# Another order of blocks, slots and banks at the two ends of a weighted expert stage

## Chip, cores, metric

One Trainium2 chip, one of its cores. The metric is the device time of one launch in microseconds (us). All arithmetic is float32.

## What is computed

An attention block gives `x` (4352 rows, 128 columns); then a layer of eight experts is applied to it, each weighted by a Sinkhorn-normalised routing matrix `P`:

```
logits = x @ w_gate;  P = exp(logits - max);  8 rounds of row and column normalisation
for e in range(E):                      # E = 8, F = 1024
    h = np.maximum(x @ w1[e], 0.0)
    ye = h @ w2[e]
    out += P[:, e:e + 1] * ye
```

The change touches only the experts, and of them only the later part, which works on inputs already multiplied by `P`.

## The kernel before

The kernel runs three stages: attention; a first expert stage under which the routing is computed (lines 772, 774, 787, 836 of the profile); and, from about 188 us on, the function `weighted()`, which the change edits.

**Groups, items, halves.** `wgroups` cuts the rows into seven groups of `2n` rows: n is 320, 480, 480, 352, 320, 224, 224. Groups 5 and 6 are the same rows; group 5 has six experts, group 6 (`LAST`, in `whole`) has the seventh alone. An item is one group with one expert, 40 in all; each is worked in two halves `s` (t counts the halves: item 0 is t = 0 and 1, group 5 is t = 66 to 77, group 6 is t = 78 and 79).

**First layer, `firsts(t)`.** `product(...)` (line 1158) issues four 64x64 matmuls, one for each quadrant of TensorE. Item 0 uses plain 2x2 blocks: four blocks of `h`, two products each, and a relu on ScalarE (line 1171) behind each block. All later items use seven products (a fast 2x2 scheme): three are copied out by ScalarE (lines 1241, 1246, 1250), three blocks are made by VectorE with an add and relu in one instruction that reads PSUM and a copy (line 1174: h0, then h2, then h3), the fourth, h1, by a ScalarE relu. Products alternate between two PSUM tiles, `pair0` and `pair1`; a product that begins a tile anew waits until its last reader is done.

**Sums of h.** For the second layer's fast scheme VectorE makes four sums, in this order: `ts0 = h3 - h0` (line 1216), `ts1 = h3 - h1` (1219), `ts2 = h1 - ts0` (1220), `ts3 = h2 - ts2` (1221). In item 0 all four stand behind the last block.

**Second layer, `seconds(t)`.** `into(...)` (line 1304) accumulates seven pairs of matmuls, four at a time, in seven slots. `tiles(rho, m, r)` is the part of row half `rho` for PSUM bank `m`: m = 0 reads h0 and h2, m = 1 reads h1 and ts0, m = 2 reads ts1 and ts2, m = 3 reads ts3. The two row halves walk the banks in different orders, so that they never stand in one bank in one slot:

```
order = ((0, 0, 2, 2, 1, 1, 3), (1, 1, 3, 0, 0, 2, 2))
```

So ts1, ts2 and ts3 are all read in slot 2 by one row half or the other.

**How the two are woven.** TensorE's order is written out: one product of `firsts(t)`, one slot of `seconds(t - 1)`, and so on; slot 0 of half t - 1 stands behind product 1 of half t, and slot 6 behind product 0 of half t + 1. VectorE, ScalarE and GpSimd each run their instructions in the order in which the program emits them; loads and stores are issued by SyncE in order.

**Small helpers around the change.** `turn` (line 1354) copies one column of a bank on ScalarE, and so makes ScalarE wait for TensorE. `aside` runs GpSimd's work for the coming items (lines 1071, 1079, 985 and others) and takes up to two pieces of work from the list `leisure`; `spare` lets VectorE take a piece in the gaps behind ts0 and behind ts3. `leisure` holds the sums that finish the previous group (`finish_seven`: eleven additions on line 1445, and two transposes with their stores, lines 1473 and 738). `ended(g, m)` copies a finished bank into `z` (line 1376); `swap_half` sends halves of `z` to the other partitions by DMA (line 1390), `begin_next_to_last` adds the near half of `z` into the result with three VectorE instructions (line 1403), `finish_next_to_last` adds the far half on GpSimd (line 1412) and once on VectorE (line 1413). Group 6 then ends the kernel: its last matmuls (line 1316), the additions on lines 1483 and 1489, transposes on 1498.

Of the kernel before, what the change touches and what calls it, by code (L numbers as in the profile page):

```python
# [14 lines left out]
Alu = mybir.AluOpType  # L15
# [37 lines left out]
def kernel(  # L53
# [12 lines left out]
    nc = tc.nc  # L66
# [14 lines left out]
    H2 = DM // 2  # L81
# [1029 lines left out]
    def weighted():  # L1111
# [14 lines left out]
        for t in range(len(todo)):  # L1126
            if t:
                a0, a1, a2, a3, a4, a5, a6 = turns[-1]
                f0, f1, f2 = unused
                now = [f0, f2, a0, a1, f1, a4, a3] if t == 1 else [f0, f1, f2, a0, a1, a4, a3]  # L1130
                unused = [a2, a5, a6]
            else:
                now, unused = unused[:7], unused[7:]
            turns.append(now)
# [7 lines left out]
        def firsts(t):  # L1142

            i, s = todo[t]
            g, e = witems[i]
            n = wgroups[g][1]
            a, c = pairs[::-1] if t % 2 and i else pairs
            w1, xf = forms[i][0], sources[i]
            h, ts = rooms(t)
            pa, pc = a[:, :, 0:n], c[:, :, 0:n]  # L1150
            p1, p5, u2 = (copies[:, m, 0:2 * n] for m in range(3))

            def product(out, form, x, start, stop):
                for r in range(2):
                    rows = slice(H2 * r, H2 * (r + 1))
                    for col in range(2):
                        o = P * s + H2 * col
                        nc.tensor.matmul(out[H2 * col:H2 * (col + 1), r], w1[rows, PLACE[form], o:o + H2], xf[rows, x],  # L1158
                                         start=start, stop=stop, tile_position=(H2 * r, H2 * col), skip_group_check=True)

            coming = next_of(i, 2) if s else None

            def fetch(lo, hi):
                if coming is not None and coming not in fresh:
                    load_first(coming, lo, hi)

            def add(out, x, y):
                nc.vector.tensor_tensor(flat(out, n), x, flat(y, n), op=Alu.add)

            def relu(x, y):  # L1170
                nc.scalar.activation(out=x, in_=y, func=Act.Relu)  # L1171

            def add_relu(out, x, y):
                nc.vector._custom_dve(TENSOR_ADD_SAT, out=flat(out, n), in0=x, in1=flat(y, n), s0=math.inf, s1=0.0)  # L1174

            def leave(engine, anywhere=False):
                if leisure and leisure[0] is None:
                    leisure.pop(0)
                elif leisure and (anywhere or leisure[0][1]):
                    leisure.pop(0)[0](engine)  # L1180
                    return True

            def gate(x, y):
                nc.scalar.copy(x, y)

            def aside(y):
# [12 lines left out]
                if s == 0 and 0 < i in fresh:  # L1199
                    store_first(i)  # L1200
                if g == 0:
                    pass
                elif chores and (s or not leisure):
                    chores.pop(0)[1]()
                else:
                    for _ in range(2 if g + 2 >= LAST else 1):
                        leave(nc.gpsimd)

            def spare(spot):
                if s == 1 and i + 1 < len(witems):  # L1210
                    sum_x(i + 1, 1 + spot)
                if 0 < g < LAST and (s == 0 or g + 1 == LAST and leisure and leisure[0] and not leisure[0][1]):
                    leave(nc.vector, True)

            def first_of_h():
                nc.vector.tensor_tensor(ts[0], h[3], h[0], op=Alu.subtract)  # L1216

            def sums_of_h():
                nc.vector.tensor_tensor(ts[1], h[3], h[1], op=Alu.subtract)  # L1219
                nc.vector.tensor_tensor(ts[2], h[1], ts[0], op=Alu.subtract)  # L1220
                nc.vector.tensor_tensor(ts[3], h[2], ts[2], op=Alu.subtract)  # L1221

            if i == 0:
                for out, (fi, ti), b in ((pa, (0, 1), 0), (pc, (1, 0), 1), (pa, (1, 1), 2), (pc, (0, 0), 3)):
                    for k in range(2):
                        product(out, 2 * k + fi, 2 * k + ti, k == 0, True)
                        yield
                        if k:
                            relu(flat(h[b], n), out)
                        if b == 0 and k:  # L1230
                            aside(h[b][:, 0:1])
                        if b == 3 and k:
                            first_of_h()
# [16 lines left out]
            nc.scalar.copy(flat(u2, n), pa)  # L1250
# [12 lines left out]
            yield  # L1263
            fetch(4, 6)
            add_relu(h[3], pc, p1)
            if g not in whole:
                first_of_h()
            spare(0)
            yield
            product(pa, 3, 7, False, True)  # L1270
            yield
            fetch(6, 7)
            relu(flat(h[1], n), pa)
            if g not in whole:
                sums_of_h()
            spare(1)
            yield

        def seconds(t):
# [20 lines left out]

            def into(rho, m, half, w, x, r):
                rows = slice(H2 * rho, H2 * (rho + 1))
                c = counts[g, m, half] = counts.get((g, m, half), 0) + 1
                nc.tensor.matmul(acc[g][m][H2 * half:H2 * (half + 1), 0:n], w[rows], flat(x, n)[rows, r],  # L1304
                                 start=c == 1, stop=True, tile_position=(H2 * rho, H2 * half),
                                 skip_group_check=True)

# [36 lines left out]
                                               ((form, 1), ts[2]))[2 * m:2 * m + 2]):  # L1344
                    into(rho, m, half, f[0](*f[1:], r), x, r)

            order = ((0, 0, 2, 2, 1, 1, 3), (1, 1, 3, 0, 0, 2, 2))
            for at in range(7):
                for rho in range(2):
                    m = order[rho ^ t % 2][at]  # L1350
                    tiles(rho, m, order[rho ^ t % 2][:at].count(m))
                yield
                for m in {1: (0, 1) if t == 0 else (0,), 3: (2,)}.get(at, ()):
                    nc.scalar.copy(turn, acc[g][m][:, 0:1])  # L1354
                for part_ in {4: (0,), 5: (1,), 6: (2, 3)}.get(at, ()):
                    fetch(part_)
                if last:
                    for m in {4: (0,), 5: (1,), 6: (2, 3)}.get(at, ()):
                        ended(g, m)
                    if at == 5:  # L1360
                        swap_half(g, 0)
                    if at == 5 and g + 1 == LAST:
                        begin_next_to_last(g)
                    if at == 6:
                        swap_half(g, 1)
                        (finish_next_to_last if g + 1 == LAST else finish_seven)(g)
                yield

        ends, swapped, loading = {}, [], [True]

        def ended(g, m):
# [4 lines left out]
            nc.scalar.copy(ends[g][:, m], acc[g][m][:, 0:n])  # L1376

        def swap_half(g, q):

# [286 lines left out]
```

## Time and profile before

| | |
|---|---|
| median of 3 runs | 888.25 us (888.14 to 888.47) |
| profiled execution, its own time | 888.43 us |
| span of the profile | 886.7 us |
| TensorE busy with matmuls | 879.2 us |
| VectorE busy | 721.7 us |
| ScalarE busy | 387.0 us |
| GpSimd busy | 259.8 us |

The span is the time from the first to the last instruction that the profile records; the rest of the execution's time, 1.7 us, lies outside it. In all rows PE is TensorE's matmuls, PEld its weight loads, DVE is VectorE, ACT ScalarE, POOL GpSimd, and SPq the DMA issues of SyncE. A row of a timeline gives the start in the span, the duration, the engine, the line of the kernel, the operation with output and inputs, the shape and the number of merged instructions; in brackets stands how long the engine had been idle before, and what ended that. One fp32 matmul shows as two records, so a product of four matmuls, or a slot, shows as x8.

### The profile page before, as it was taken

How to read it: one execution, taken by the hardware profiler on the slowest of the kernel's cores; microseconds unless marked ns; L12 is line 12 of the kernel's file. 1: busy time of each engine (PE TensorE's matmuls, PEld its weight loads, DVE VectorE, ACT ScalarE, POOL GpSimd, SP SyncE). 2: the span in 40 equal slices, each digit the busy share in tenths (PEclk: the TensorE clock that was granted, in tenths of full speed). 3: DMA queues.
4: the chain of work that ended last, by engine and by line, in shares of the span. 5: the costliest groups of instructions: out<-in, count | busy, mean ns of one | idle time of the engine just before them, and what ended most of it. 6: DMA issues, size and time to landing. Idle time of an engine off the chain costs nothing.

```text
span 886.7 us, 26215 instructions
## 1 busy us (share of the span) xinstructions
PE 879.2 (99%) x10828; PEld 568.1 (64%) x10828; DVE 721.7 (81%) x981; ACT 387.0 (44%) x817; POOL 259.8 (29%) x253
## 2 busy tenths in 40 slices
PE   9999999999999999999999999999999999999998
PEld 6788656855867656666555555555444566667786
DVE  8699689977888877788877778888788888888986
ACT  3455557544444533333343333334344344445443
POOL 3131125353532213222222222221333333311411
PEclk9999999999999999999999999999999999999999
DMA  8889399786666554454435444434755557566671
GB/s 262 266 272 280 78 232 246 123 261 178 197 190 197 175 167 129 136 142 123 127 99 145 137 125 126 122 107 114 191 146 160 148 133 223 147 181 194 199 209 36
DMA packets 120887, 149.08 MB, mean 168 GB/s; under 512 B 52288, under 2 KB 79808, under 8 KB 120384
## 3 DMA queue, kind: packets, MB, share of 16 engines
q1 hardware_dynamic: 112656, 136.92, 54.4%
q0 software_dynamic: 6720, 10.19, 5.8%
q8 instruction: 86, 1.41, 0.7%
q10 hardware_dynamic: 1392, 0.28, 0.2%
q14 instruction: 33, 0.27, 0.1%
HBM read 104.86 MB, written 25.99 MB: 148 GB/s over the span
## 4 chain that ended last, share of the span: by engine, by line
PE 97%; DVE 2%; ACT 0%; issue 0%; POOL 0%; DVEq 0%; ACTq 0%; POOLq 0%
PE s L1304 38%; PE pair L1158 38%; PE a L772 9%; PE s L836 7%; PE a L336 1%; PE a L465 1%; PE a L120 1%; PE a L306 0%; DVE hb L1221 0%; DVE hb L1219 0%; DVE hb L1220 0%; PE s L375 0%; PE a L429 0%; PE s L395 0%; DVE hb L1216 0%; PE s L1316 0%
## 5 line engine op out<-in xcount | busy, mean ns | idle before, releaser
L1158 PE MATMUL pair<-xf,w1x 64*64 64x320 f32 (+3 forms) x4496 | 570.2, 466 | 0.6 <-DVE hb L1174 0.6
L1304 PE MATMUL s<-hb,w 64*64 64x480 f32 (+3 forms) x2544 | 368.2, 466 | 0.1
L1158 PEld LDWEIGHTS pair<-xf,w1x 64*64 64x64 f32 x4496 | 250.3, 133 | 120.2 <-issue 77.5
L1174 DVE CUSTOM_DVE_ANT_0 hb<-pair,copies 128x960 f32<-128x960 f32 (+3 forms) x234 | 214.7, 918 | 101.8 <-PE pair L1158 92.5
L1304 PE MATMUL s<-hb,ws 64*64 64x480 f32 (+3 forms) x1888 | 286.8, 469 | 1.5 <-DVE hb L1221 1.0
L1304 PEld LDWEIGHTS s<-hb,w 64*64 64x64 f32 x2544 | 152.9, 133 | 78.1 <-issue 51.8
L1304 PEld LDWEIGHTS s<-hb,ws 64*64 64x64 f32 x1888 | 115.0, 133 | 61.4 <-issue 37.9
L1071 POOL TENSOR_TENSOR xf<-xT,pb 128x960 f32<-128x960 f32 (+3 forms) x40 | 70.0, 1750 | 245.5 <-ACT turn L1354 186.9
L1079 POOL TENSOR_TENSOR xf<-xf 128x960 f32<-128x960 f32 (+3 forms) x39 | 68.0, 1743 | 229.1 <-ACT turn L1354 168.4
L1171 ACT ACTIVATE hb<-pair 128x640 f32<-128x640 f32 (+3 forms) x86 | 66.4, 772 | 136.7 <-PE pair L1158 136.0
L772 PE MATMUL a<-xT,w 128*64 128x416 f32 (+3 forms) x512 | 122.9, 465 | 0.0
L1354 ACT COPY turn<-s 128x1 f32<-128x1 f32 x157 | 24.5, 156 | 155.0 <-PE s L1304 154.8
L774 ACT ACTIVATE hb<-a 128x416 f32<-128x416 f32 (+3 forms) x128 | 59.5, 468 | 65.8 <-PE a L772 60.6
L1216 DVE TENSOR_TENSOR hb<-hb 128x960 f32<-128x960 f32 (+3 forms) x78 | 75.1, 963 | 12.8 <-ACT hb L1171 4.9
L1221 DVE TENSOR_TENSOR hb<-hb 128x960 f32<-128x960 f32 (+3 forms) x78 | 72.5, 930 | 8.4 <-DVE hb L1220 0.5
L1219 DVE TENSOR_TENSOR hb<-hb 128x960 f32<-128x960 f32 (+3 forms) x78 | 73.2, 938 | 2.8 <-ACT hb L1171 1.3
L1250 ACT COPY copies<-pair 128x960 f32<-128x960 f32 (+3 forms) x78 | 59.8, 767 | 35.5 <-PE pair L1158 35.5
L1246 ACT COPY copies<-pair 128x960 f32<-128x960 f32 (+3 forms) x78 | 60.0, 770 | 33.1 <-PE pair L1158 33.1
L1241 ACT COPY copies<-pair 128x960 f32<-128x960 f32 (+3 forms) x78 | 59.8, 767 | 32.8 <-PE pair L1158 28.9
L1220 DVE TENSOR_TENSOR hb<-hb 128x960 f32<-128x960 f32 (+3 forms) x78 | 71.9, 922 | 0.0
L836 PE MATMUL s<-hb,ws 128*64 128x416 f32 (+3 forms) x224 | 71.6, 474 | 0.0
L787 DVE TENSOR_TENSOR hb<-hb 128x416 f32<-128x416 f32 (+7 forms) x84 | 57.2, 684 | 12.6 <-ACT hb L774 9.7
(203 smaller groups left out, 659.0 us busy)
## 6 DMA issues: line engine op xcount, KB each, us to landing
w1x<-w1x SPq DMA_DIRECT2D x87, 256.0 KB, 3.4
w<-w2x SPq DMA_DIRECT2D x71, 256.0 KB, 3.2
ws<-w2x SPq DMA_DIRECT2D x35, 256.0 KB, 3.3
pb<-pT SPq DMA_DIRECT2D x14, 480.0 KB, 3.8
xf<-xf SPq DMA_DIRECT2D x28, 240.0 KB, 3.3
w1x<-w1x SPq DMA_DIRECT2D x7, 896.0 KB, 5.9
ws<-w2x SPq DMA_DIRECT2D x36, 128.0 KB, 3.4
pb<-pT SPq DMA_DIRECT2D x13, 320.0 KB, 3.7
```

The lines of the kernel that those rows point to most:

```text
L772: nc.tensor.matmul(ph[sl], loaded_w[j][0][:, P * f + H2 * s:P * f + H2 * (s + 1)], xT[:, at + lo:at + hi], start=True, stop=True, tile_pos ...
L836: nc.tensor.matmul(sums[g][i][H2 * s:H2 * (s + 1)], w, x, start=c == 1, stop=c == per, tile_position=(0, H2 * s))
L1071: nc.gpsimd.tensor_tensor(xf[:, 0:2].rearrange("p b n -> p (b n)"), xT[:, lo:lo + 2 * n], weights.pop(i), op=Alu.mult)
L1079: nc.gpsimd.tensor_tensor(xf[:, 4:6], xf[:, 1:4:2], xf[:, 0:2], op=Alu.subtract)
L1158: nc.tensor.matmul(out[H2 * col:H2 * (col + 1), r], w1[rows, PLACE[form], o:o + H2], xf[rows, x], start=start, stop=stop, tile_position=(H ...
L1171: nc.scalar.activation(out=x, in_=y, func=Act.Relu)
L1174: nc.vector._custom_dve(TENSOR_ADD_SAT, out=flat(out, n), in0=x, in1=flat(y, n), s0=math.inf, s1=0.0)
L1216: nc.vector.tensor_tensor(ts[0], h[3], h[0], op=Alu.subtract)
L1219: nc.vector.tensor_tensor(ts[1], h[3], h[1], op=Alu.subtract)
L1220: nc.vector.tensor_tensor(ts[2], h[1], ts[0], op=Alu.subtract)
L1221: nc.vector.tensor_tensor(ts[3], h[2], ts[2], op=Alu.subtract)
L1304: nc.tensor.matmul(acc[g][m][H2 * half:H2 * (half + 1), 0:n], w[rows], flat(x, n)[rows, r], start=c == 1, stop=True, tile_position=(H2 * r ...
```

## The change

Three edits, all in `weighted()`.

1. In item 0 the blocks of `h` come in the order h3, h0, h1, h2 (before: h0, h1, h2, h3), and each sum stands right behind the last block that it needs: ts0 behind h0, ts1 and ts2 behind h1, ts3 behind h2. The buffers of t = 1 are assigned anew to suit.
2. A group with `2n <= 512` that is not in `whole` (only group 5) takes the slots in the plain order 0, 0, 1, 1, 2, 2, 3 in both row halves. Each row half has two banks of its own, in which two of the `m` lie side by side; the two are added when the group ends: `ended` copies one bank of 2n columns on ScalarE and adds the other to it on VectorE (a new instruction on line 1394 of the changed kernel). The `turn` copies are left out in these groups, and the loads of the next weights (`fetch`) come as soon as the plain order is done with the old ones.
3. In group 5 `spare` lets VectorE take only transposes from `leisure`; the additions are left to GpSimd.

```diff
-                now = [f0, f2, a0, a1, f1, a4, a3] if t == 1 else [f0, f1, f2, a0, a1, a4, a3]
+                now = [f1, a4, f0, f2, a0, a1, a3] if t == 1 else [f0, f1, f2, a0, a1, a4, a3]
...
-                if 0 < g < LAST and (s == 0 or g + 1 == LAST and leisure and leisure[0] and not leisure[0][1]):
+                if 0 < g < LAST and (leisure and leisure[0] and not leisure[0][1] if g + 1 == LAST else s == 0):
                     leave(nc.vector, True)
...
-                for out, (fi, ti), b in ((pa, (0, 1), 0), (pc, (1, 0), 1), (pa, (1, 1), 2), (pc, (0, 0), 3)):
+                for out, (fi, ti), b in ((pa, (0, 0), 3), (pc, (0, 1), 0), (pa, (1, 0), 1), (pc, (1, 1), 2)):
...
-                        if b == 0 and k:
-                            aside(h[b][:, 0:1])
-                        if b == 3 and k:
-                            first_of_h()
-                            sums_of_h()
-                            for part_ in (() if s else (1, 2)):
-                                sum_x(1, part_)
+                            if b == 3:
+                                aside(h[b][:, 0:1])
+                            for do in {0: (first_of_h,), 1: (next_of_h,), 2: (last_of_h,)}.get(b, ()):
+                                do()
+                            if b == 2:
+                                for part_ in (() if s else (1, 2)):
+                                    sum_x(1, part_)
...
-                c = counts[g, m, half] = counts.get((g, m, half), 0) + 1
-                nc.tensor.matmul(acc[g][m][H2 * half:H2 * (half + 1), 0:n], w[rows], flat(x, n)[rows, r],
+                bank_ = (2 * rho + m // 2, half) if narrow(g) and g not in whole else (m, half)
+                c = counts[(g, *bank_)] = counts.get((g, *bank_), 0) + 1
+                out_ = acc[g][m][:, 0:n]
+                if narrow(g) and g not in whole:
+                    out_ = acc[g][2 * rho + m // 2][:, n * (m % 2):n * (m % 2 + 1)]
+                nc.tensor.matmul(out_[H2 * half:H2 * (half + 1)], w[rows], flat(x, n)[rows, r],
...
-            order = ((0, 0, 2, 2, 1, 1, 3), (1, 1, 3, 0, 0, 2, 2))
+            order = ((0, 0, 1, 1, 2, 2, 3),) * 2 if narrow(g) else ((0, 0, 2, 2, 1, 1, 3), (1, 1, 3, 0, 0, 2, 2))
+            full = [max(k for line in order for k in range(7) if line[k] == m) for m in range(4)]
...
-                for m in {1: (0, 1) if t == 0 else (0,), 3: (2,)}.get(at, ()):
-                    nc.scalar.copy(turn, acc[g][m][:, 0:1])
-                for part_ in {4: (0,), 5: (1,), 6: (2, 3)}.get(at, ()):
-                    fetch(part_)
+                if not narrow(g):
+                    for m in {1: (0, 1) if t == 0 else (0,), 3: (2,)}.get(at, ()):
+                        nc.scalar.copy(turn, acc[g][m][:, 0:1])
+                for m in range(4):
+                    if full[m] == at:
+                        fetch(m)
+                        if last:
+                            ended(g, m)
                 if last:
-                    for m in {4: (0,), 5: (1,), 6: (2, 3)}.get(at, ()):
-                        ended(g, m)
-                    if at == 5:
-                        swap_half(g, 0)
-                    if at == 5 and g + 1 == LAST:
-                        begin_next_to_last(g)
+                    for q in range(2):
+                        if at == max(full[2 * q:2 * q + 2]):
+                            swap_half(g, q)
+                            if q == 0 and g + 1 == LAST:
+                                begin_next_to_last(g)
...
-            nc.scalar.copy(ends[g][:, m], acc[g][m][:, 0:n])
+            if not narrow(g):
+                nc.scalar.copy(ends[g][:, m], acc[g][m][:, 0:n])
+            elif m % 2:
+                z = ends[g][:, m - 1:m + 1].rearrange("p m n -> p (m n)")
+                nc.scalar.copy(z, acc[g][m // 2][:, 0:2 * n])
+                nc.vector.tensor_tensor(z, acc[g][2 + m // 2][:, 0:2 * n], z, op=Alu.add)
```

More of the change, by code (lines that the diff above doesn't have):

```diff
@@ L1216, in first_of_h, with next_of_h, last_of_h @@
                 nc.vector.tensor_tensor(ts[0], h[3], h[0], op=Alu.subtract)
-            def sums_of_h():
+            def next_of_h():
                 nc.vector.tensor_tensor(ts[1], h[3], h[1], op=Alu.subtract)
                 nc.vector.tensor_tensor(ts[2], h[1], ts[0], op=Alu.subtract)
+            def last_of_h():
                 nc.vector.tensor_tensor(ts[3], h[2], ts[2], op=Alu.subtract)
             if i == 0:
-                for out, (fi, ti), b in ((pa, (0, 1), 0), (pc, (1, 0), 1), (pa, (1, 1), 2), (pc, (0, 0), 3)):
+                for out, (fi, ti), b in ((pa, (0, 0), 3), (pc, (0, 1), 0), (pa, (1, 0), 1), (pc, (1, 1), 2)):
                     for k in range(2):
@@ L1274, in firsts @@
             if g not in whole:
-                sums_of_h()
+                next_of_h()
+                last_of_h()
             spare(1)
@@ L1352, in seconds @@
                 yield
-                for m in {1: (0, 1) if t == 0 else (0,), 3: (2,)}.get(at, ()):
-                    nc.scalar.copy(turn, acc[g][m][:, 0:1])
-                for part_ in {4: (0,), 5: (1,), 6: (2, 3)}.get(at, ()):
-                    fetch(part_)
-                if last:
-                    for m in {4: (0,), 5: (1,), 6: (2, 3)}.get(at, ()):
-                        ended(g, m)
-                    if at == 5:
-                        swap_half(g, 0)
-                    if at == 5 and g + 1 == LAST:
-                        begin_next_to_last(g)
+                if not narrow(g):
[6 more added lines that the diff above has]
+                            ended(g, m)
+                if last:
+                    for q in range(2):
[3 more added lines that the diff above has]
+                                begin_next_to_last(g)
                     if at == 6:
-                        swap_half(g, 1)
                         (finish_next_to_last if g + 1 == LAST else finish_seven)(g)
@@ L1369, in weighted, with narrow @@
         ends, swapped, loading = {}, [], [True]
+        def narrow(g):
+            return 2 * wgroups[g][1] <= 512
         def ended(g, m):
```

## The prediction

> **What bounds the kernel now.** I read the page first: where the time is, and what the chain that ended last is made of.
>
> ```profile
> PE 879.2 (99%) x10828; PEld 568.1 (64%) x10828; DVE 721.7 (81%) x981; ACT 387.0 (44%) x817; POOL 259.8 (29%) x253
> PE 97%; DVE 2%; ACT 0%; issue 0%; POOL 0%; DVEq 0%; ACTq 0%; POOLq 0%
> ```
>
> TensorE sets the end, and the change neither adds nor removes one matmul. All that it can win is the time in which TensorE stands still or half filled. The chain says who causes that: VectorE. So I went to the chain in the stretch of item 0 (start, duration, what).
>
> ```profile
> 193.84 0.84 DVE hb L1216
> 194.70 1.31 DVE hb L1219
> 196.01 1.28 DVE hb L1220
> 197.32 1.24 DVE hb L1221
> 198.60 0.49 PE s L1304 x2
> ...
> 207.32 0.77 PE s L1304 x8
> 208.09 0.54 PE pair L1158 x8
> ...
> 213.47 0.53 PE pair L1158 x7
> ```
>
> From 208.09 to 213.47 ten undisturbed pieces (products and slots in turn) take 5.38 us, 0.538 each. Before that the four sums run one behind the other, and a slot starts only when the last is done, at 198.60 and again at 207.32. Three rows of the timeline more, for the start of item 0 and its relus, and three of GpSimd:
>
> ```profile
> 188.47 5.64 PE L1158 MATMUL pair<-xf,w1x 64*64 64x320 f32 x80
> ...
> 190.92 0.70 ACT L1171 ACTIVATE hb<-pair 128x640 f32<-128x640 f32 x1 [0.32 <-PE pair L1158]
> ...
> 191.97 1.55 POOL L1079 TENSOR_TENSOR xf<-xf 128x640 f32<-128x640 f32 x1 [3.23 <-DMA xf<-xf]
> 192.02 0.70 ACT L1171 ACTIVATE hb<-pair 128x640 f32<-128x640 f32 x1 [0.40 <-PE pair L1158]
> ...
> 193.10 0.70 ACT L1171 ACTIVATE hb<-pair 128x640 f32<-128x640 f32 x1 [0.37 <-PE pair L1158]
> ...
> 194.60 0.73 POOL L985 TENSOR_TENSOR w1x<-w1x 128x256 f32<-128x256 f32 x1 [1.08 <-DMA w1x<-in_moe_w_dram]
> 195.29 1.31 POOL L984 TENSOR_TENSOR w1x<-w1x 128x256 f32<-128x256 f32 x1
> ```
>
> Slot 2 behind the second half of item 0 starts at 207.32. Ahead of it lie, from 188.47, 20 products (8 of t = 0, 8 of t = 1, 4 of t = 2) and 9 slots (7 and 2). That is 29 pieces x 0.538 = 15.60 us, and 18.85 went by: **3.25 us are lost in item 0**.
>
> Group 5 the same way, with the timeline around its first slot, its last halves, and the places where it stumbles:
>
> ```profile
> 807.53 0.56 PE L1304 MATMUL s<-hb,w 64*64 64x224 f32 x8
> ...
> 821.16 0.86 POOL L1445 TENSOR_TENSOR w<-w,z 64x320 f32<-64x320 f32 x1
> ...
> 821.58 0.62 DVE L1174 CUSTOM_DVE_ANT_0 hb<-pair,copies 128x448 f32<-128x448 f32 x1 [0.20 <-PE pair L1158]
> ...
> 822.10 0.87 POOL L1445 TENSOR_TENSOR m<-m,w 64x320 f32<-64x320 f32 x1
> 822.31 1.13 DVE L1216 TENSOR_TENSOR hb<-hb 128x448 f32<-128x448 f32 x1
> ...
> 831.56 1.31 DVE L1445 TENSOR_TENSOR z<-m,f 64x320 f32<-64x320 f32 x1
> 832.91 1.16 DVE L1174 CUSTOM_DVE_ANT_0 hb<-pair,copies 128x448 f32<-128x448 f32 x2
> ...
> 865.18 2.03 DVE L1174 CUSTOM_DVE_ANT_0 hb<-pair,copies 128x448 f32<-128x448 f32 x3 [0.54 <-ACT turn L1354]
> ...
> 866.34 0.56 PE L1304 MATMUL s<-hb,w 64*64 64x224 f32 x8
> ...
> 869.37 0.56 PE L1304 MATMUL s<-hb,w 64*64 64x224 f32 x8
> ...
> 869.96 0.38 DVE L1083 TENSOR_TENSOR xf<-xf 128x224 f32<-128x224 f32 x1
> ...
> 873.93 0.73 PE L1304 MATMUL s<-hb,w 64*64 64x224 f32 x6
> ```
>
> From 866.34 to 869.37 lie eight pieces, 0.379 each. From slot 0 of the group's first half (807.53) to slot 0 of group 6 (873.93) lie 12 halves x 14 = 168 pieces, 63.6 us; 66.4 went by: **2.8 us are lost in group 5**. A half with no piece of `leisure` keeps VectorE from 865.18 to 870.34, 5.16 us, and TensorE's 14 pieces take 5.30. So an odd half leaves VectorE 0.14 us, and any addition of line 1445 makes it late; the worst place is the addition of 1.31 us at 831.56, which holds back the add-relu at 832.91.
>
> **The change part by part.**
>
> *Item 0.* The sums are the same four for each half, in the same order; only their places move. ts0 may start behind h0's relu (190.92 + 0.70 = 191.62), ts1 and ts2 behind h1's (192.72), ts3 behind h2's (193.80). Slot 0 now starts at 193.85 without ts0 late, and slot 2 is due four pieces later, at 196.0; it wants ts1 and ts2, then ts3 at about 196.1. Alone (0.84 each, row of 193.84) the sums would end at 195.2, no wait. But GpSimd works from 191.97 on, and beside it the same sums took 1.24 to 1.31. Taking GpSimd's turns as they come: ts0 to 192.5, ts1 behind line 1079 to 194.7, ts2 behind line 985 to 196.0, ts3 behind line 984 to about 197.1: a wait of 1.0. Bounds: 0 and 1.7 (all four at 1.31 and one more turn). The second half has over two pieces more to spare and should not wait; one relu there waits for slot 4, which has just been reading the buffer, and is early enough. So **-2.25** (-3.25 to -1.55).
>
> *Group 5.* Four additions go from VectorE to GpSimd, which then does eleven of 0.87 in a group of 66 us; its own queue has room. Two transposes stay. The plain order asks for h1 and ts0 in slot 2, ts1 and ts2 in slot 4, ts3 in slot 6: ts3 gets four slots, 3.0 us, more than in slot 2. What stays is one VectorE sum held up for about 0.5 us (1.13 at 822.31 for 0.62) in each half with two additions on GpSimd, of which there are now four, not two; behind an odd half this leaves the next add-relu 0.4 late. The pair that it frees is wanted two pieces and a product later, so I leave 0.3 us of the 2.8. **-2.5** (-2.8 to -1.7). For matmuls that share a bank by columns, and row halves that read the same operand, no row of slots stands here; line 1158 runs both row halves on the same x at the same 0.379, so I take nothing for it. Leaving out `turn`, and earlier weight loads, cost nothing: ScalarE is 44% busy. Stores of group 4 go out later on SyncE's queue, between loads that are two items ahead; without that cover a store would hold the queue for a transpose, half a microsecond.
>
> *Into group 5.* The second row half now starts in bank 2, not bank 1. The rows below show the copies of banks 2 and 3 at 807.37; bank 2 is free near 807.8, and its matmuls are due at 807.72. **+0.15** (0 to 0.4).
>
> *Out of group 5.* Here something new stands in VectorE's queue.
>
> ```profile
> 807.37 0.76 ACT L1376 COPY z<-s 128x320 f32<-128x320 f32 x2
> ...
> 869.62 0.53 ACT L1250 COPY copies<-pair 128x448 f32<-128x448 f32 x1 [0.22 <-PE pair L1158]
> ...
> 870.48 2.06 DVE L1174 CUSTOM_DVE_ANT_0 hb<-pair,copies 128x448 f32<-128x448 f32 x3
> ...
> 871.11 0.36 PE L1304 MATMUL s<-hb,ws 64*64 64x224 f32 x2
> ...
> 872.80 0.56 PE L1158 MATMUL pair<-xf,w1x 64*64 64x224 f32 x8
> ...
> 873.47 3.21 SPq L1390 DMA_DIRECT2D w<-z  x4
> 873.48 1.18 DVE L1403 TENSOR_TENSOR kept<-kept,z 64x224 f32<-64x224 f32 x3 [0.95 <-ACT z L1376]
> ...
> 874.26 0.14 PEld L1304 LDWEIGHTS s<-hb,w 64*64 64x64 f32 x2 [0.18 <-ACT z L1376]
> ...
> 878.60 0.66 POOL L1412 TENSOR_TENSOR m<-m,w 128x224 f32<-128x224 f32 x1
> ...
> 880.04 0.39 DVE L1489 TENSOR_TENSOR kept<-kept,w 128x224 f32<-128x224 f32 x1 [0.23 <-POOL w L1412]
> ...
> 881.11 0.39 DVE L1483 TENSOR_TENSOR kept<-s,kept 128x224 f32<-128x224 f32 x1 [0.38 <-PE s L1316]
> ```
>
> In the plain order the first half of `z` is complete behind slot 3, not slot 5. In the changed program VectorE therefore has, between the add-relus of h2 and h3 of t = 78, the new addition of two banks and the three instructions of line 1403, which used to stand behind h3. Slot 3 ends at 871.47 (last row at 871.11 + 0.36). The copy of 448 columns takes 0.53 (as on line 1250), to 872.0; the addition of 128x448 from PSUM does not stand in the trace, its neighbours take 0.62 (line 1216 undisturbed) and 0.69 (line 1174), I take 0.65, to 872.65; line 1403 1.18, to 873.85; h3's add-relu 0.69, to 874.55. Product 0 of t = 79 begins the same pair anew, is queued on TensorE behind nothing else, and was due at 872.80: it starts near 874.6, 1.8 late, and every matmul behind it with it. The old wait for bank 2 at 874.26, 0.2, goes. **+1.6** (0.8 if slot 3 or the copy is early, 2.2).
>
> *The tail.* The second half of `z` is ready 0.6 later still than TensorE's delay explains, but before it was SyncE's queue, four issues in 3.21, that set the landing at 878.60. I get the GpSimd additions 0.2 later relative to TensorE, and the idle 0.38 ahead of 881.11 covers that. **0** (to +0.5).
>
> The sum: -2.25 - 2.5 + 0.15 + 1.6 + 0 = **-3.0 us**. Against the profiled execution's 888.43 (span 886.7 and 1.7 outside it) that is 885.4; that execution is 0.2 above the median 888.25, so **885.3 us**. Its ends: -3.25 - 2.8 + 0 + 0.8 = -5.25 and -1.55 - 1.7 + 0.4 + 2.2 + 0.5 = -0.15.
>
> **A rule of the Trainium skill.** At 822.31 VectorE's sum took 1.13, and GpSimd's addition ended at 822.97: the sum looks held until then. The Trainium skill, SBUF — State Buffer, section Who interferes with whom, says that a VectorE instruction with two SBUF inputs and a GpSimd instruction that reads SBUF exclude each other for the whole instruction, the first to issue going first. By that rule the trace agrees, and it speaks against moving additions to GpSimd: each can stop a sum for its full length.
>
> **Rivals.**
>
> *A, no new wait.* The chain out of group 5 is hidden, or item 0's sums run alone: -3.0 less 1.6, about -4.6, 883.7. Against it: the order of VectorE's queue is in the program, and GpSimd's rows of 194.60 and 195.29 are not moved by the change. 0.12.
>
> *B, the sums stay late.* GpSimd costs item 0 its full 1.7, and group 5 keeps half of its loss: -1.55 - 1.4 + 0.15 + 1.6 = -1.2, 887.1. For it: the 1.24 to 1.35 of the sums beside GpSimd. 0.13.
>
> *C, slower: GpSimd takes VectorE's time in group 5.* All eleven additions stop VectorE for their length, 11 x 0.87 = 9.5 us. Free on VectorE are 0.14 in an odd half and, without the two 0.38 of sum_x (869.96), 0.9 in an even one, 3.1 in the six halves. 6.4 is then lost in place of 2.8: +3.6 - 1.55 + 1.75 = +3.8, 892.0. It decides the sign once the additions stop VectorE for over 0.53 us each. Against it: the addition at 821.16 lay beside an add-relu that took its 0.62 all the same (821.58), and only the one at 822.10 cost VectorE 0.5; GpSimd's pieces begin with the add-relus of a half, so most of their length falls there. 0.05.
>
> **How the numbers follow.** The forecast has 0.68, the rivals 0.12, 0.13 and 0.05, and 0.02 goes to the unforeseen, slower. 0.2% of the time, 1.8 us, is what a measurement can tell here. The range 883.5 to 887.1 holds the forecast's ends but the last microsecond on either side that its parts reach only all together, A's middle and B's. Faster than 886.45: nearly all of the forecast (0.65), A, a quarter of B: 0.80. Same: the rest of both, 0.13. Slower: C and the unforeseen, 0.07.
>
> **What would show it.** Right: in the changed trace ts0 starts near 191.7 and no sum ends a wait near 207; group 5's additions on line 1445 are all on POOL, and its 168 pieces take about 64; one PE wait of line 1158 for DVE line 1174 of 1 to 2 us stands at the first product of t = 79, with the three instructions of line 1403 just ahead of that add-relu. Wrong: sums of 1.3 us and waits for ts3 still in item 0 (B), PE waits for line 1174 spread through group 5 (C), slots slower than 0.379, or no wait at t = 79 (A).

## The result and the profile after

| | before | after |
|---|---|---|
| median of 11 runs each | 888.33 us (887.51 to 889.65) | 885.89 us (885.55 to 886.69) |
| ratio | | 0.9972 (95%: 0.9963 to 0.9982) |
| profiled execution, its own time | 888.43 us | 885.63 us |
| span | 886.7 us | 883.9 us |

The change saves 2.4 us; 3.0 were forecast, and the time lies inside the range. From line 1221 on, lines of the changed kernel are 2 to 18 higher than before: 1221 is 1223 now, 1304 is 1311, 1376 is 1390 (1393 for the copy of 2n columns), 1403 is 1421, 1412 is 1430, 1445 is 1463, 1483 is 1501. In the kernels of the experiments they differ by a few more (1393 to 1403 for 1393 and 1394, 1463 to 1472 for 1463).

The busy times and the chain of work that ended last, from the page of the changed kernel:

```profile
PE 877.1 (99%) x10828; PEld 576.8 (65%) x10828; DVE 723.0 (82%) x979; ACT 384.6 (44%) x791; POOL 263.8 (30%) x257
PE 99%; DVE 0%; ACT 0%; issue 0%; POOL 0%; POOLq 0%
```

VectorE's 2% have left the chain. To see where, I cut each trace at three starts: the first product of item 0, the first product of 480 columns (the end of group 0), and slot 0 of group 5. Before, these are 188.47 and 807.53, shown above, and this row of the timeline:

```profile
294.04 0.57 PE L1158 MATMUL pair<-xf,w1x 64*64 64x480 f32 x2
```

After:

```profile
188.72 5.61 PE L1158 MATMUL pair<-xf,w1x 64*64 64x320 f32 x80
...
291.80 0.57 PE L1158 MATMUL pair<-xf,w1x 64*64 64x480 f32 x2
...
805.31 0.72 PE L1311 MATMUL s<-hb,w 64*64 64x224 f32 x6
```

Stretch A, item 0 and the rest of group 0, goes from 105.57 to 103.08 us, **-2.49**. The middle stays (513.49 and 513.51). Stretch C, from slot 0 of group 5 to the end of the span, goes from 79.1 to 78.5, **-0.6**. What precedes `weighted()` took 0.25 longer in this execution. That is the whole of 888.43 to 885.63.

**Item 0.** VectorE's timeline, with GpSimd's rows, and one row of the chain:

```profile
191.30 1.81 DVE L688 TENSOR_TENSOR kept<-x,m 64x416 f32<-64x416 f32 x1
193.03 0.81 DVE L1216 TENSOR_TENSOR hb<-hb 128x640 f32<-128x640 f32 x1
193.94 0.82 DVE L1219 TENSOR_TENSOR hb<-hb 128x640 f32<-128x640 f32 x1
194.69 0.82 DVE L1220 TENSOR_TENSOR hb<-hb 128x640 f32<-128x640 f32 x1
195.61 1.20 DVE L1223 TENSOR_TENSOR hb<-hb 128x640 f32<-128x640 f32 x1
...
191.12 1.54 POOL L1079 TENSOR_TENSOR xf<-xf 128x640 f32<-128x640 f32 x1 [2.34 <-DMA xf<-xf]
...
195.40 0.73 POOL L985 TENSOR_TENSOR w1x<-w1x 128x256 f32<-128x256 f32 x1 [2.75 <-DMA w1x<-in_moe_w_dram]
```

```profile
205.21 0.54 PE s L1311 x8
```

205.21 is slot 2 behind the second half, 29 pieces after 188.72: 16.49 - 15.60 = 0.89 lost, where 3.25 were lost before. The sums are no longer one block at the end. But ts0 does not start near 191.7: line 688, the last instruction of the stage before, is ahead of it in VectorE's queue and took 1.81.

**Group 5.** Two of its places where a sum lies beside an addition on GpSimd, the first in an odd half, the second in an even one, each with a GpSimd row first; between them a row of the chain, the late product behind the odd half, 0.61 for an undisturbed 0.38. Then the exit (ScalarE's copy, VectorE, TensorE):

```profile
820.21 1.31 POOL L1463 TENSOR_TENSOR m<-w,z 64x320 f32<-64x320 f32 x1
...
820.71 1.06 DVE L1081 TENSOR_TENSOR xf<-xf 128x224 f32<-128x224 f32 x1
...
824.39 0.61 PE pair L1158 x8
...
825.69 0.86 POOL L1463 TENSOR_TENSOR m<-m,w 64x320 f32<-64x320 f32 x1
...
825.73 1.31 DVE L1216 TENSOR_TENSOR hb<-hb 128x448 f32<-128x448 f32 x1
```

```profile
867.34 0.53 ACT L1393 COPY z<-s 128x448 f32<-128x448 f32 x1 [1.31 <-PE s L1311]
...
866.29 1.28 DVE L1174 CUSTOM_DVE_ANT_0 hb<-pair,copies 128x448 f32<-128x448 f32 x2 [0.26 <-PE pair L1158]
867.90 0.62 DVE L1394 TENSOR_TENSOR z<-s,z 128x448 f32<-128x448 f32 x1 [0.33 <-ACT z L1393]
868.56 1.18 DVE L1421 TENSOR_TENSOR kept<-kept,z 64x224 f32<-64x224 f32 x3
869.67 0.61 DVE L1174 CUSTOM_DVE_ANT_0 hb<-pair,copies 128x448 f32<-128x448 f32 x1
...
868.21 0.56 PE L1311 MATMUL s<-hb,ws 64*64 64x224 f32 x8
870.33 0.61 PE L1158 MATMUL pair<-xf,w1x 64*64 64x224 f32 x8 [1.56 <-DVE hb L1174]
...
871.52 0.56 PE L1311 MATMUL s<-hb,w 64*64 64x224 f32 x8
```

Product 0 of t = 79 was due one piece after 868.21, at 868.59, and started at 870.33: **a new wait of 1.74 us** (the 1.56 in brackets is TensorE's idle time alone). The 168 pieces of group 5 (805.31 to 871.52) take 66.21, as long as before (66.40), because of it; without it 64.47 against an undisturbed 63.63, so 0.84 is lost where 2.77 were. By the starts of TensorE's pieces these 0.84 lie in three places: 0.27 at the entry (the slot eight pieces behind slot 0 starts at 808.61, 3.30 and not 3.03 later), and about 0.3 each at the products of 824.39 and 835.25, behind the two odd halves with a held-up sum. The two sums held up in even halves (the one at 825.73 and another at 836.58) cost TensorE nothing.

### The profile page after: what moved, and what is told of

Same layout as the page of the kernel before. It is cut to its first block, busy times and chain, and to the rows that moved or that the text cites. A ratio compares the mean times of both kernels' runs of the same rounds, so it can differ in the third digit from the quotient of the medians.

```text
span 883.9 us, 26160 instructions
## 1 busy us (share of the span) xinstructions
PE 877.1 (99%) x10828; PEld 576.8 (65%) x10828; DVE 723.0 (82%) x979; ACT 384.6 (44%) x791; POOL 263.8 (30%) x257
## 4 chain that ended last, share of the span: by engine, by line
PE 99%; DVE 0%; ACT 0%; issue 0%; POOL 0%; POOLq 0%
PE pair L1158 39%; PE s L1311 39%; PE a L772 9%; PE s L836 7%; PE a L336 1%; PE a L465 1%; PE a L120 1%; PE a L306 0%; PE s L375 0%; PE a L429 0%; PE s L395 0%; PE s L1323 0%; PE a L499 0%; PE a L375 0%; DVE kept L1421 0%; PE a L395 0%
## 5 line engine op out<-in xcount | busy, mean ns | idle before, releaser
L1158 PE MATMUL pair<-xf,w1x 64*64 64x320 f32 (+3 forms) x4496 | 576.5, 466 | 1.6 <-DVE hb L1174 1.6
L1311 PE MATMUL s<-hb,w 64*64 64x480 f32 (+3 forms) x2544 | 364.0, 466 | 0.0
L1158 PEld LDWEIGHTS pair<-xf,w1x 64*64 64x64 f32 x4496 | 254.9, 133 | 117.4 <-issue 64.0
L1174 DVE CUSTOM_DVE_ANT_0 hb<-pair,copies 128x960 f32<-128x960 f32 (+3 forms) x234 | 214.7, 918 | 102.5 <-PE pair L1158 90.1
L1311 PE MATMUL s<-hb,ws 64*64 64x480 f32 (+3 forms) x1888 | 280.9, 468 | 0.0
L1363 ACT COPY turn<-s 128x1 f32<-128x1 f32 x133 | 20.7, 156 | 137.2 <-PE s L1311 137.2
```

The costliest lines, as they stand in the source:

```text
L1311: nc.tensor.matmul(out_[H2 * half:H2 * (half + 1)], w[rows], flat(x, n)[rows, r], start=c == 1, stop=True, tile_position=(H2 * rho, H2 * h ...
```

## The experiments

All kernels, with stretches A and C of each trace; each ratio is to runs of the kernel before beside it (medians 888.08 to 888.33). The middle is 513.5 in all of them, so a difference comes from A, from C or from the stages before, whose end (the first product of item 0) lies between 188.47 and 189.18 in traces in which that code is the same. Kernels with the same code in A differ there by up to 0.5, and in C by 0.3; below that a stretch tells nothing.

| kernel | median, us | ratio to before (95%) | A | C |
|---|---|---|---|---|
| before | 888.33 | | 105.57 | 79.1 |
| after | 885.89 | 0.9972 (0.9963 to 0.9982) | 103.08 | 78.5 |
| edit 1 alone | 886.68 | 0.9982 (0.9973 to 0.9990) | 103.02 | 79.1 |
| edits 2 and 3 | 887.87 | 0.9994 (0.9986 to 1.0003) | 105.93 | 78.5 |
| edit 2 alone | 889.03 | 1.0009 (1.0000 to 1.0018) | 105.49 | 80.0 |
| edit 3 alone | 887.42 | 0.9991 (0.9983 to 1.0000) | 105.58 | 78.4 |
| three instructions behind h3 | 884.79 | 0.9961 (0.9948 to 0.9973) | 103.24 | 77.3 |
| four behind h3 | 883.80 | 0.9950 (0.9936 to 0.9963) | 102.83 | 76.7 |
| the same, banks exchanged | 883.41 | 0.9944 (0.9931 to 0.9956) | 103.09 | 76.4 |
| additions twice | 892.37 | 1.0049 (1.0035 to 1.0063) | 103.34 | 85.9 |
| out of the way | 884.11 | 0.9952 (0.9938 to 0.9966) | 102.53 | 77.7 |
| first sum on VectorE | 883.12 | 0.9945 (0.9932 to 0.9959) | 102.41 | 76.7 |

### Edit 1 alone

The first and third hunk of the change, and `sums_of_h` split in two; all else as before.

> Edit 1 alone on the kernel before: item 0's blocks in the order h3, h0, h1, h2, each sum behind its block; group 5 as before. Theory (the parts are separate): item 0 gives its 2.5 us whole and nothing downstream takes it back, 888.3 - 2.5 = 885.8; slot 0 of group 5 comes 2.2 to 2.5 earlier than before, and group 5 loses its old 2.8. Rival (the gain is given back later: loads or sums that are now due 2.5 earlier make TensorE wait somewhere in groups 0 to 6): 886.5 to 888, with the excess in a named stretch.

886.68, 0.9 above the theory's number and inside the rival's range; but the trace has A at 103.02, 2.55 below before, and the middle and C unchanged (513.5 and 79.1), so that no stretch has the rival's excess. In the trace item 0 gives its 2.5 and nothing takes it back. Why the medians show only 1.5 (0.9 to 2.4 by the interval) is not shown; it would lie ahead of `weighted()`, or in the scatter of the runs.

### Edits 2 and 3, and each alone

All three have item 0 as before. The first has both other edits whole; edit 2 alone has this line besides, as it was before:

```diff
-                if 0 < g < LAST and (leisure and leisure[0] and not leisure[0][1] if g + 1 == LAST else s == 0):
+                if 0 < g < LAST and (s == 0 or g + 1 == LAST and leisure and leisure[0] and not leisure[0][1]):
```

Edit 3 alone is that line reversed, on the kernel before.

> Edits 2 and 3 alone, item 0 as before. Theory: group 5's slots lose about 0.8 in place of 2.8 (a gain of 2.0), the old wait for bank 2 goes (0.3), and the new wait of product 0 of t = 79 for h3's add-relu takes 1.8 back: -0.5 net, 887.8 (887.4 to 888.2). Rival 1 (group 5 gains nothing of its own and item 0 made all of the change): 888.3 + 1.5 = 889.8, above before. Rival 2 (the wait of 1.8 came only because item 0 ran early): no wait at t = 79, 886.1.

> Edit 2 alone (plain order and own banks in group 5); item 0 and the additions as before, so VectorE again takes a share of line 1445. Theory (group 5 gains by both: sums that may be later, and an engine that is less loaded): slots of group 5 lose 1.3 to 2.0, between the 2.8 of before and the 0.8 of edits 2 and 3 together, and the wait of 1.6 to 1.8 at t = 79 stays: 888.2 - 1.2 + 0.2 + 1.5 = 888.7. Rival 1 (the order alone gives it all): 887.9, as with edits 2 and 3. Rival 2 (the additions on VectorE are all of it): 890.

> Edit 3 alone (additions of line 1445 all on GpSimd in group 5); item 0, order and banks as before, so there is no new wait at t = 79. Theory: VectorE is no longer late with add-relus, but a sum held up by GpSimd is still read in slot 2; group 5 loses 1.0 to 1.8 in place of 2.8: 886.8. Rival 1 (GpSimd holds up VectorE as long as it relieves it): 888.2, PE waits for the sums of lines 1219 to 1221 in group 5. Rival 2 (the additions on VectorE are all of the loss): 0.8 lost, 886.2.

Both together: 887.87, C -0.6, with the wait of 1.6 at t = 79 although nothing runs early. The traces bear out the theory, and both its rivals fall (889.8, and no wait); the median by itself is not told apart from before (0.9986 to 1.0003).

Edit 2 alone is slower than before in its trace, C +0.9, and in its median just so (0.8, with an interval that begins at 1.0000): the theory's 1.3 to 2.0 lost was too hopeful. The wait at t = 79 is in this kernel too, 1.51 at 874.04; without it (1.7 by the starts) C would be about 0.8 below before, which is an estimate, as that kernel was not run. Its timeline has the place that the prediction had marked as the worst, an addition on VectorE in an odd half, as before:

```profile
831.69 1.31 DVE L1464 TENSOR_TENSOR z<-m,f 64x320 f32<-64x320 f32 x1
833.03 1.16 DVE L1174 CUSTOM_DVE_ANT_0 hb<-pair,copies 128x448 f32<-128x448 f32 x2
...
833.71 0.61 PE L1158 MATMUL pair<-xf,w1x 64*64 64x224 f32 x8 [1.53 <-DVE hb L1174]
```

TensorE waits 1.53 for the add-relu that the addition holds back; its matmuls wait for no sum in this group any more. The plain order gives sums more time, but an add-relu none.

Edit 3 alone, C -0.7: less than the theory, and the waits of TensorE say what is left. Each line gives the total wait in us, the number of waits and the longest; first group 5 before, then with edit 3 alone:

```profile
PE pair L1158 <- DVE hb L1174: 0.6, 1, 0.6
PE s L1304 <- DVE hb L1221: 0.5, 2, 0.3
...
PE s L1304 <- DVE hb L1221: 0.8, 3, 0.4
```

The wait for an add-relu (1174) is gone. Those for ts3 (1221) are not: the old order reads ts2 and ts3 in slot 2, and when GpSimd holds up ts0, the sums behind it are late there. That is the wait of its rival 1, though the rival's time (888.2) is not reached.

So each edit removes the wait that the other leaves: the order lets sums be late, the additions on GpSimd let add-relus be on time. Together, without the new wait (next experiment), they are worth 2.4 in C.

### Behind h3: all four instructions, or three

In the changed kernel, the addition of the two banks, the exchange of z's first half and line 1421 are emitted one slot later (at slot 4); or `begin_next_to_last`, line 1421, alone. The diff is of the first of these kernels; `add_banks` is the addition that it takes out of `ended`.

```diff
-                nc.vector.tensor_tensor(z, acc[g][2 + m // 2][:, 0:2 * n], z, op=Alu.add)
...
                 if last:
+                    if narrow(g) and at in (4, 6):
+                        add_banks(g, 1 if at == 4 else 3)
                     for q in range(2):
-                        if at == max(full[2 * q:2 * q + 2]):
+                        if at == (max(full[2 * q:2 * q + 2]) if not narrow(g) else (4, 6)[q]):
```

> The changed kernel with the addition of the two banks, the exchange of z's first half and the three instructions of line 1403 (1421 after) emitted one slot later, behind h3's add-relu. Theory (the wait at t = 79 is the place of these four instructions in VectorE's queue): h3's add-relu ends near 868.7 and not 870.3, product 0 of t = 79 starts when due, 885.9 - 1.8 = 884.1; the additions finish early enough for group 6's banks. Rival (the time is spent somewhere else all the same: group 6's first slots wait for bank 2, which now is read later, or the last exchange comes later and the tail waits for it): 885 to 886, with a wait for the bank addition at slot 0 of group 6 or for line 1430 at the end.

> The changed kernel with only the three instructions of line 1403 (1421 after) emitted one slot later, behind h3's add-relu; the addition of the two banks stays ahead of it. Theory (the wait at t = 79 is these instructions' time, each at its own length): 1.18 of the 1.8 goes and about 0.6 stays for the bank addition, 885.9 - 1.2 = 884.7, with a wait of 0.3 to 0.6 on line 1174 at product 0 of t = 79. Rival (the bank addition, which waits for ScalarE's copy, holds the queue by itself): the wait stays above 1, 885.3 to 885.9.

All four: 883.80, 2.1 below after, C -1.8, and no wait of TensorE on line 1174 is left. VectorE's queue is the same work in another order:

```profile
866.02 2.04 DVE L1174 CUSTOM_DVE_ANT_0 hb<-pair,copies 128x448 f32<-128x448 f32 x3 [0.27 <-PE pair L1158]
867.97 0.61 DVE L1400 TENSOR_TENSOR z<-s,z 128x448 f32<-128x448 f32 x1
868.62 1.18 DVE L1427 TENSOR_TENSOR kept<-kept,z 64x224 f32<-64x224 f32 x3
```

Three of them: 884.79, 1.1 below after, where 1.2 was expected, and one wait of TensorE is left:

```profile
PE pair L1158 <- DVE hb L1174: 0.3, 1, 0.3
```

The wait is the length of what stands ahead of the add-relu, piece by piece: C falls by 1.2 without line 1421 there, and by 0.6 more without the bank addition. That the banks are read later and the exchange starts later cost nothing that shows: from slot 0 of group 6 to the end it is 12.3 to 12.4 us in all these kernels.

### Banks exchanged on entry

```diff
-                acc[g] = [mps.tile([P, 512], F32, tag=f"s{m}", name="s") for m in range(4)]
+                acc[g] = [mps.tile([P, 512], F32, tag=f"s{m}", name="s") for m in ((0, 2, 1, 3) if narrow(g) else range(4))]
```

> The kernel with the four instructions behind h3, and in groups 5 and 6 the second row half's first bank is the one that group 4 leaves a slot earlier (bank 1 for bank 2). Theory: the wait for a bank on entry to group 5 (0.15 to 0.27) goes and nothing else moves: 883.9, 0.2 below the same kernel without it. Rival: bank 1 is free no earlier in practice, since its copy on ScalarE stands behind others: no difference.

883.41, 0.4 below; the runs overlap (883.51 to 884.39 without it, 882.99 to 883.92 with it). The wait itself was there in the changed kernel, on weight loads, and is gone here:

```profile
805.62 0.14 PEld L1311 LDWEIGHTS s<-hb,w 64*64 64x64 f32 x2 [0.17 <-ACT z L1390]
```

The starts of TensorE's pieces show what it is worth in the trace: from slot 0 to the slot eight pieces on it is 3.02 us here (805.73 to 808.75) and was 3.30 in the changed kernel, and eight undisturbed pieces take 3.03. The rival, no difference, falls there; the medians do not show it.

### The additions twice

```diff
-                leisure.append((lambda engine: engine.tensor_tensor(own(k, rows), of(a), of(b), op=op), True))
+                def do(engine):
+                    engine.tensor_tensor(own(k, rows), of(a), of(b), op=op)
+                    if g + 2 == LAST and k not in (a, b):
+                        engine.tensor_tensor(own(k, rows), of(a), of(b), op=op)
+
+                leisure.append((do, True))
```

> The changed kernel with eight of the eleven GpSimd additions of group 5 done twice (the same sum into the same place), 7 us more of GpSimd's time in group 5. Theory (an addition costs TensorE only where it meets a sum, and most of its length lies beside add-relus, which read PSUM): +0.3 to +1.0, 886.5. Rival (rival C of the prediction, GpSimd stops VectorE for its length whatever VectorE runs): 7 us less what is free on VectorE in these halves, +2.5 to +5, 888.4 to 891. If additions beside sums cost nothing: 885.9.

892.37: the theory's size falls, and the rival's upper end is passed; C is 7.3 longer for 7 us more of GpSimd. The timeline of one half (GpSimd, VectorE, TensorE):

```profile
818.14 1.14 POOL L1079 TENSOR_TENSOR xf<-xf 128x448 f32<-128x448 f32 x1 [1.91 <-ACT xf L1184]
819.24 0.86 POOL L1464 TENSOR_TENSOR m<-z,w 64x320 f32<-64x320 f32 x1
820.18 0.86 POOL L1466 TENSOR_TENSOR m<-z,w 64x320 f32<-64x320 f32 x1
821.11 1.13 POOL L1464 TENSOR_TENSOR m<-w,z 64x320 f32<-64x320 f32 x1
822.32 0.89 POOL L1466 TENSOR_TENSOR m<-w,z 64x320 f32<-64x320 f32 x1
...
818.12 2.04 DVE L1174 CUSTOM_DVE_ANT_0 hb<-pair,copies 128x448 f32<-128x448 f32 x3 [0.20 <-ACT xf L1184]
820.19 1.33 DVE L1216 TENSOR_TENSOR hb<-hb 128x448 f32<-128x448 f32 x1
821.44 1.05 DVE L1081 TENSOR_TENSOR xf<-xf 128x224 f32<-128x224 f32 x1
822.42 1.28 DVE L1219 TENSOR_TENSOR hb<-hb 128x448 f32<-128x448 f32 x1
...
824.27 1.59 DVE L1223 TENSOR_TENSOR hb<-hb 128x448 f32<-128x448 f32 x1
825.78 1.04 DVE L1083 TENSOR_TENSOR xf<-xf 128x224 f32<-128x224 f32 x1
...
827.41 0.61 PE L1158 MATMUL pair<-xf,w1x 64*64 64x224 f32 x8 [2.31 <-DVE hb L1174]
```

While VectorE runs its three add-relus (2.04, as without GpSimd) GpSimd's pieces cost nothing. From 820.19 on both have work waiting, and they take turns: five of the six sums take 0.7 to 1.0 longer than their 0.62 (0.38 on lines 1081 and 1083; line 1220 at 823.62 keeps its 0.61), 3.7 in this half, where the prediction found 0.14 to spare. TensorE waits 2.3 for the next add-relu, and in a second half 2.8. So the theory's mechanism stands, since the add-relus are not held up and the rival's "whatever VectorE runs" is wrong; but a held-up sum costs nearly its whole delay once the room is gone. What keeps the changed kernel out of this part of the prediction's rival C is that seven of its eleven additions end about when the add-relus do; the other four, each the second in its half, hold up one sum each.

### GpSimd out of the way of the sums

On the kernel with the banks exchanged, first both edits, then the first alone:

```diff
-        sum_x(1, 0)
...
+                                    nc.vector.tensor_tensor(x1[:, 4:6], x1[:, 1:4:2], x1[:, 0:2], op=Alu.subtract)
...
-                    for _ in range(2 if g + 2 >= LAST else 1):
+                    for _ in range(2 if g + 2 >= LAST and (s or g + 1 < LAST) else 1):
```

> The kernel with the four instructions behind h3 and the banks exchanged, and two edits more that only take GpSimd out of VectorE's way: item 1's first sum of x (line 1079, 1.5 to 2.1 us on GpSimd beside the sums of item 0) is made by VectorE behind ts3; and in group 5 GpSimd takes one addition, not two, in every other half, so that none runs on into the sums. Theory (what is left in both places is sums held up by a GpSimd instruction already running): item 0 loses 0.1 in place of 0.4 to 0.8, group 5 0.2 in place of 0.5 to 0.8: 883.4 - 0.9 = 882.5, with all of item 0's sums at 0.82. Rival 1 (the loss is in the time of the copies and relus, not in the sums): 883.4. Rival 2 (the spread additions end so late that the stores of group 4 stand ahead of the last loads or of the exchange on SyncE's queue): 884 or more, with a PE wait for a DMA in group 6 or a later line 1430.

> The kernel with the four instructions behind h3 and the banks exchanged, and only item 1's first sum of x made by VectorE behind ts3 instead of by GpSimd (line 1079) beside item 0's sums; GpSimd's additions in group 5 as in the changed kernel. Theory: item 0's 0.56 is kept without the loss that spreading the additions brought to group 5, 883.4 - 0.5 = 882.9, item 0 losing 0.1 to 0.2 and group 5 0.8. Rival (the loss in group 5 of the run before came from the earlier start of group 5, not from spreading the additions): 883.9 to 884.1, with group 5 losing 1.2 or more.

Item 0 does what the theory says, in both: A 102.53 and 102.41, 0.6 below 103.1. The four sums in the last kernel (the fifth, which VectorE has taken over, follows at 195.31 and takes 0.82 too):

```profile
191.75 0.83 DVE L1216 TENSOR_TENSOR hb<-hb 128x640 f32<-128x640 f32 x1
192.83 0.83 DVE L1219 TENSOR_TENSOR hb<-hb 128x640 f32<-128x640 f32 x1 [0.25 <-ACT hb L1171]
193.57 0.82 DVE L1220 TENSOR_TENSOR hb<-hb 128x640 f32<-128x640 f32 x1
194.49 0.82 DVE L1223 TENSOR_TENSOR hb<-hb 128x640 f32<-128x640 f32 x1
```

They start at 191.75, the 191.7 of the prediction, and end before slot 2. So about 0.6 of the 0.89 that item 0 still lost in the changed kernel hung on line 1079. What lines 985 and 984 cost ts3 is among it: with line 1079 gone from GpSimd, ts3 ends before line 985 begins, at 195.55. The medians of this kernel and the one without the edit (883.12 and 883.41) do not show the 0.6; their runs overlap.

Spreading the additions made C longer, against the theory: 77.7, by 0.9 beside the last kernel (76.7), which starts as early and differs in this alone. So it was the spreading and not the earlier start. Rival 2 falls too: no wait for a DMA shows in group 6, and behind its slot 0 the kernel takes 12.3 us like the others. The starts of the pieces say where the 0.9 lies. Spread in this way, the four pairs of additions all fall into odd halves, which have next to no room, and the product behind each is late: at 823.32, 834.18, 845.09 and 856.32. In the last kernel, as in the changed one, two of the four pairs fall into even halves, and only two products are late (823.19 and 834.04). The product of 845.09 costs 0.3 and that of 856.32 costs 0.6, which together are the 0.9. The latter is the worst because the transpose of line 1500 (0.50 at 853.23), later than before, comes into such a half:

```profile
851.72 1.28 DVE L1216 TENSOR_TENSOR hb<-hb 128x448 f32<-128x448 f32 x1
...
856.32 0.61 PE L1158 MATMUL pair<-xf,w1x 64*64 64x224 f32 x8 [0.41 <-DVE hb L1174]
```

Pairs in even halves alone were not tried. The last kernel, 883.12, is with the one that has only the banks exchanged (883.41) the fastest of all, 5.0 us below before (888.08 beside it) and 2.8 below the change; between the two no difference is shown.

## Why the prediction was right

- **Item 0, -2.25.** A gave -2.49, alone -2.55. The size is right, in part by luck, since the step under it was not: the 1.0 that it left was to be ts3 behind lines 985 and 984. These came later, at 195.40 and 196.09, and cost ts3 0.4 (1.20 at 195.61). The larger part was line 1079, which came 0.85 earlier than before (191.12, not 191.97), ahead of line 688, and held that up for 1.2; ts0 then waited in VectorE's queue. The prediction had not looked at what stands ahead of ts0, and took line 1079's start as fixed. In the kernel with four instructions behind h3, with the same code here, line 1079 started 0.88 later, line 688 took its 0.58, and line 1079 held up ts1 instead, as the prediction had it:

```profile
191.29 0.58 DVE L688 TENSOR_TENSOR kept<-x,m 64x416 f32<-64x416 f32 x1
...
192.97 1.84 DVE L1219 TENSOR_TENSOR hb<-hb 128x640 f32<-128x640 f32 x1 [0.25 <-ACT hb L1171]
...
192.00 2.12 POOL L1079 TENSOR_TENSOR xf<-xf 128x640 f32<-128x640 f32 x1 [3.13 <-DMA xf<-xf]
```

- **Group 5, -2.5, and into it, +0.15.** Together -2.35 was forecast. 2.77 lost became 0.84 with the entry in it, -1.9. This term was mis-sized by 0.4: the prediction saw one sum held up in each half with two additions, which is what the trace shows (four sums, 0.7 each), but took the next add-relu's lateness behind an odd half as all but hidden. It was not: two such halves cost about 0.3 each where 0.3 was left for all, and the entry cost 0.27 where 0.15 was taken. For the plain order itself nothing was taken, and nothing came: its undisturbed slots and products keep their 0.379.
- **Out of group 5, +1.6.** 1.74 came for 1.8, at the product and behind the four instructions that it named, with the bank addition at 0.62 (0.65 taken), line 1421 at 1.18, the add-relu at 0.61 (0.69). The stretch behind slot 0 of group 6 (from 871.52 to the end, 883.9; before 873.93 to 886.7) is 0.4 shorter, where 0.2 for the old wait for bank 2 was reckoned.
- **The tail, 0.** It came out as 0, though its step did not: GpSimd's addition `m<-m,w` stands 4.09 us behind slot 0 of group 6 (at 875.61), 0.6 earlier than before (4.67) where 0.2 later was forecast. VectorE's last wait is for TensorE as before, 0.59 where it was 0.38:

```profile
878.33 0.39 DVE L1501 TENSOR_TENSOR kept<-s,kept 128x224 f32<-128x224 f32 x1 [0.59 <-PE s L1323]
```

- **The sum.** -2.49 - 1.9 + 1.74 - 0.4 is -3.05 for `weighted()`, where -3.0 was forecast; errors of 0.2 to 0.5 of both signs cancel. The medians show 0.6 less than that. The profiled execution's own 0.25 ahead of `weighted()` is a part of it, and the rest lies within the scatter of the runs (885.55 to 886.69).
- **The rivals.** A falls by the wait at t = 79, B by sums of 0.81 and 0.82. C did not come in the changed kernel, and the runs lie on both sides of its point of decision, eleven stops of 0.53 or 5.8 us: in the changed kernel four sums are held up by 0.7, 2.8 us, and the sign stays; with the additions twice eleven instructions are held up, 7.6 us in all, and it turns. That this kernel's 892.37 is near C's 892.0 is chance, as it has eight additions more than C reckoned with.
- **The rule of the Trainium skill**, SBUF — State Buffer, section Who interferes with whom, says one thing more than the prediction took from it: a VectorE instruction with at most one SBUF input, outside the 2-port perf modes, does not contend with GpSimd. The traces agree: the add-relu, with one input in PSUM, takes 2.04 for three beside GpSimd (818.12 above) and without it (855.70 in the changed kernel). They agree on the order of issue too: line 1079 first (191.12) holds up line 688 (191.30, 1.81 for 0.58); in the kernel with the additions twice line 688 is first (191.06, 0.58) and line 1079 is held up (191.10, 1.96 for 1.54).

## What to carry to other kernels

A wait is made by what stands ahead in an engine's queue: when work that finishes a group is moved forward, walk the queue to the next instruction that TensorE waits for, and emit the new work behind that one (here 2.1 us of 4.4). Two repairs of one stretch can be worth little alone and much together, if each leaves the wait that the other removes. Work handed to GpSimd was free here as long as it lay beside VectorE instructions that read PSUM, or held up sums in a half where VectorE had room; beyond that both engines took turns, and the price went from about 0.6 us for eleven additions to 7.3 us for eight more.

## What the runs showed of the hardware

When VectorE (two SBUF inputs) and GpSimd both have work queued, they alternate one by one, and each instruction's record grows: sums of 0.62 show 1.10 to 1.59, sums of 0.38 show 1.04 to 1.06, additions of 0.86 show up to 1.31 (820.21 in the changed kernel). The profile shows this as busy time, not as a wait. When line 1079 starts differs between traces of the same code, from 191.1 to 193.1, with the end of the transfer that its row names; so does what it holds up, line 688, ts0 or ts1. What it costs differs little: A is 102.8 to 103.3 in these six traces, and 102.4 to 102.5 where it is taken off GpSimd.
